# Gated scan and two MLPs on one core: the streamed weights move up by 160 bytes in SBUF

## The chip, the core and the metric

The kernel runs on one core of a Trainium2 chip. The metric is the device time of one execution in microseconds (us), lower is better. PE is the matrix engine (TensorE), PEld its weight loads, DVE the VectorE, ACT the ScalarE, SP the SyncE, whose queue issues the DMAs. SBUF is the on-chip memory of 128 partitions from which the engines read; an address here is a byte offset within each partition. PSUM is the memory of eight banks into which PE sums.

## The reference

```python
# x, f_logit: (2, 6080, 256); lower_bound: (256,); two MLPs with w_in (256, 2048), w_out (2048, 256)
sig = 1.0 / (1.0 + np.exp(-f_logit))
f = lower_bound + (1.0 - lower_bound) * sig
h[t] = f[:, t] * h[t - 1] + (1.0 - f[:, t]) * x[:, t]        # the scan: y[:, t] = h[t]
...
y1 = np.maximum(y @ w_in1, 0.0) ** 2 @ w_out1                # 12160 tokens
h2 = y1 @ w_in2
out = np.where(h2 > 0.0, h2, np.exp(np.minimum(h2, 0.0)) - 1.0) @ w_out2
```

## The kernel before

The 12160 tokens are cut into 12 units: the first of 512 + 384 tokens, the second of 512 + 512, ten more of 512 + 512. A unit is scanned, goes through MLP 1 (m = 0), is written to DRAM (`xd`), read back and goes through MLP 2 (m = 1) two units later. The work of one unit in one MLP is a run; a run has eight slots, one for each group g of 256 of the 2048 inner columns.

All products are of fp32 accuracy from fp32r parts: each operand is split into a high and a low part, and a product is three matmuls, high x high, high x low, low x high (`three`, lines 631 to 636). The first two units of MLP 1 take a slot as plain products, 12 matmuls for each half of the unit (`add_plain`). All later runs save an eighth of the input products with a seven-product scheme for blocks of two by two: `add_first` issues three products (9 matmuls, right operand `xa`), `add_later` four (12 matmuls, right operand `xb`), and ACT and DVE add the results up into `r`. Every matmul of an input product is at line 633, its left operand (the weights) lies in a tile `ws`, which for the seven products holds 2 parts x 7 blocks x 128 columns of fp32 in each partition, 7168 bytes. The pool of `ws` has two buffers; a tile is loaded for each slot by one DMA of 896 KB from the DRAM copy `wd` (`add_stream`, line 472). In the plain slots the weights stand alternately in a `ws` tile (its first four blocks) and in a tile of the pool `s` (`plain_weights`, line 323).

The second product of each MLP, the output sums (line 855), has its weights in SBUF for good: `wo[m]`, 32768 bytes a partition each. Its right operand is `g`, the activated `r`, split by ACT (line 673) and DVE (line 678). A slot of the seven-product runs is therefore four blocks on PE: 9 matmuls of c from xa and ws, 12 of a from g and wo, 12 of c from xb and ws, 12 of a from g and wo, 45 in all; nearly all have 512 columns, the runs of MLP 2's first unit 448.

The order of the work on each engine is fixed when the program is built: the class `Order` plays it through with estimated durations and due times and writes the instructions in that order. Addresses play no part in it. PE's order of blocks comes from `pe_order`. In PSUM each of the four accumulators c0 to c3 has one bank: the next slot's product may begin once ACT or DVE have read the last one (c3 by line 804, `mid_even`).

SBUF is laid out by the order in which the pools are opened, one behind the other, every buffer rounded up to a multiple of 32 bytes. The first 1152 bytes belong to a scratch area and to four constants that every program has. Behind them stood so far the two `ws` buffers, then the pool `const` with five small tiles (lb, ga, gb, carry of 8 bytes, warm of 4) and the two `wo`, then the other pools. lb, ga, gb, carry and warm are the lower bound, the two coefficients of the gate, the state carried between scans and a tile that serves to load a table at the start.

Of the kernel before, what the change touches and what calls it, by code (L numbers as in the profile page):

```python
# [8 lines left out]
F32R = mybir.dt.float32r  # L9
# [6 lines left out]
P = 128  # L16
# [10 lines left out]
BUFS = {  # L27
# [3 lines left out]
}  # L31
# [119 lines left out]
def kernel(  # L151
# [12 lines left out]
    B, S, D = x.shape  # L164
# [3 lines left out]
    KF = DFF // P  # L168
# [6 lines left out]
    PLAIN = len(SIZES)  # L175
    starts = [sum(map(sum, units[:u])) for u in range(NU)]

    pools = {"ws": ctx.enter_context(tc.tile_pool(name="ws_pool", bufs=BUFS["ws"]))}
    const = ctx.enter_context(tc.tile_pool(name="const", bufs=1))
    lb = const.tile([P, KD], F32, name="lb")  # L180
    ga = const.tile([P, KD], F32, name="ga")
    gb = const.tile([P, KD], F32, name="gb")
    carry = const.tile([P, KD], F32, name="carry")
    warm = const.tile([P, 1], F32, name="warm")
    wo = [const.tile([P, KF, 2, D], F32R, name=f"wo{m}") for m in range(2)]
    pools |= {
        tag: ctx.enter_context(tc.tile_pool(name=f"{tag}_pool", bufs=n))
        for tag, n in BUFS.items()
# [67 lines left out]
    for s in slots:  # L256
        m, u, h, g = s
# [702 lines left out]
    for kind, s in pe_order:  # L960
# [3 lines left out]
        m, u, h, g = s  # L964
# [52 lines left out]
```

## Time and profile before

| | |
|---|---|
| median of three runs | 2049.47 us (2049.08 to 2049.62) |
| the profiled execution | 2049.94 us, its span 2048.2 us |
| mean granted PE clock | 0.993 |
| busy share of the span: PE, DVE, ACT | 97%, 82%, 80% |
| DMA | 267.30 MB, 131 GB/s over the span |

The page and the views come from one profiled execution. Times are counted from the start of its span. A row of the timeline merges equal instructions that follow each other: its start, the time from there to the end of the last one, and their number (x12). Matmuls are pipelined, so the end of a block overlaps the start of the next; the time that a block takes on PE is the distance from its start to the next start. Releasers of waits are inferred from semaphore events.

### The profile page before, as it was taken

How to read it: one execution, taken by the hardware profiler on the slowest of the kernel's cores; microseconds unless marked ns; L12 is line 12 of the kernel's file. 1: busy time of each engine (PE TensorE's matmuls, PEld its weight loads, DVE VectorE, ACT ScalarE, POOL GpSimd, SP SyncE). 2: the span in 40 equal slices, each digit the busy share in tenths (PEclk: the TensorE clock that was granted, in tenths of full speed). 3: DMA queues.
4: the chain of work that ended last, by engine and by line, in shares of the span. 5: the costliest groups of instructions: out<-in, count | busy, mean ns of one | idle time of the engine just before them, and what ended most of it. 6: DMA issues, size and time to landing. Idle time of an engine off the chain costs nothing.

```text
span 2048.2 us, 24509 instructions
## 1 busy us (share of the span) xinstructions
PE 1995.6 (97%) x8688; PEld 1633.5 (80%) x8688; DVE 1676.1 (82%) x2285; ACT 1638.2 (80%) x2170; POOL 0.2 (0%) x4
## 2 busy tenths in 40 slices
PE   5999969999999999999999999999999999999998
PEld 4887958888888888888888888888888888888886
DVE  6878997788889779879878888977987987857886
ACT  6988967887888788888788788878888878878885
POOL 0000000000000000000000000000000000000000
PEclk9999989999999999999999999999999999999999
DMA  7877744324324334333432432433433333233231
GB/s 191 240 245 241 230 129 128 131 91 142 125 94 137 99 132 131 111 131 114 128 131 90 143 125 93 137 99 131 132 110 132 114 108 131 91 111 118 94 105 54
DMA packets 235138, 267.30 MB, mean 131 GB/s; under 512 B 160008, under 2 KB 160776, under 8 KB 235016
## 3 DMA queue, kind: packets, MB, share of 16 engines
q1 hardware_dynamic: 234432, 265.21, 41.3%
q8 instruction: 68, 1.11, 0.2%
q10 hardware_dynamic: 584, 0.53, 0.1%
q14 instruction: 54, 0.44, 0.1%
HBM read 221.91 MB, written 43.78 MB: 130 GB/s over the span
## 4 chain that ended last, share of the span: by engine, by line
PE 90%; DVE 4%; ACT 2%; DMA 2%; issue 1%; SPq 1%; DVEq 0%; ACTq 0%
PE a L855 47%; PE c L633 43%; DVE g L678 1%; DMA a<-rd 1%; DMA fs<-in_f_logit_dram 1%; ACT g L673 1%; SPq L566 0%; ACT r L658 0%; ACT a L369 0%; DMA st<-in_moe_w_in_dram 0%; ACT r L725 0%; DVE a L375 0%; DVE a L378 0%; DVE F L602 0%; DVE a L339 0%
## 5 line engine op out<-in xcount | busy, mean ns | idle before, releaser
L855 PE MATMUL a<-g,wo 128*128 128x512 f32 (+1 forms) x4608 | 1107.1, 389 | 0.9 <-DVE g L678 0.9
L855 PEld LDWEIGHTS a<-g,wo 128*128 128x128 f32 x4608 | 865.2, 188 | 184.5 <-DVE g L678 1.3
L678 DVE TENSOR_TENSOR g<-r,g 128x1024 fp32r<-128x1024 f32 (+2 forms) x384 | 463.2, 1206 | 169.4 <-ACT g L673 168.4
L633 PE MATMUL c<-xb,ws 128*128 128x512 f32 (+2 forms) x2208 | 540.4, 393 | 0.0
L673 ACT ACTIVATE g<-r 128x1024 fp32r<-128x1024 f32 (+2 forms) x384 | 403.4, 1050 | 134.7 <-PE a L855 121.8
L633 PEld LDWEIGHTS c<-xb,ws 128*128 128x128 f32 x2208 | 414.7, 188 | 94.2
L633 PE MATMUL c<-xa,ws 128*128 128x512 f32 (+1 forms) x1680 | 427.6, 398 | 44.2 <-ACT xa L482 35.7
L633 PEld LDWEIGHTS c<-xa,ws 128*128 128x128 f32 x1680 | 318.1, 190 | 122.1 <-ACT xa L482 36.1
L756 ACT ACTIVATE s<-c 128x512 f32<-128x512 f32 (+1 forms) x528 | 307.3, 588 | 7.3 <-PE c L633 7.3
L668 DVE SCALAR_TENSOR_TENSOR r<-e,r 128x1024 f32<-128x1024 f32 (+1 forms) x192 | 232.1, 1209 | 34.3 <-ACT e L665 34.3
L662 ACT ACTIVATE e<-r 128x1024 f32<-128x1024 f32 (+1 forms) x192 | 201.5, 1049 | 39.8 <-DVE r L800 37.0
L658 ACT ACTIVATE r<-r 128x1024 f32<-128x1024 f32 x192 | 201.7, 1051 | 2.3
L665 ACT ACTIVATE e<-e 128x1024 f32<-128x1024 f32 (+1 forms) x192 | 201.4, 1049 | 1.5
L796 ACT ACTIVATE r<-c 128x512 f32<-128x512 f32 (+1 forms) x176 | 104.0, 591 | 106.1 <-PE c L633 106.0
L760 DVE TENSOR_TENSOR s<-s 128x512 f32<-128x512 f32 (+1 forms) x176 | 119.9, 681 | 74.2 <-ACT s L756 74.0
L793 DVE TENSOR_TENSOR s<-c,s 128x512 f32<-128x512 f32 (+1 forms) x176 | 120.6, 685 | 39.9 <-PE c L633 38.9
L804 DVE TENSOR_TENSOR r<-c,s 128x512 f32<-128x512 f32 (+1 forms) x176 | 119.5, 679 | 4.4
L800 DVE TENSOR_TENSOR r<-c,s 128x512 f32<-128x512 f32 (+1 forms) x176 | 119.8, 680 | 2.2
L807 DVE TENSOR_TENSOR r<-s 128x512 f32<-128x512 f32 (+1 forms) x176 | 119.1, 677 | 0.0
L652 ACT ACTIVATE r<-r 128x1024 f32<-128x1024 f32 x80 | 84.4, 1055 | 3.5 <-DVE r L807 3.5
L655 ACT ACTIVATE r<-r 128x512 f32<-128x512 f32 x80 | 50.4, 630 | 30.7 <-DVE r L800 30.7
L602 DVE TENSOR_TENSOR_SCAN F<-fT,carry,xT 128x256 f32<-128x256 f32 (+2 forms) x94 | 65.3, 723 | 1.2
(47 smaller groups left out, 759.0 us busy)
## 6 DMA issues: line engine op xcount, KB each, us to landing
ws<-wd SPq DMA_DIRECT2D x176, 896.0 KB, 4.9
fs<-in_f_logit_dram SPq DMA_DIRECT2D x184, 64.0 KB, 2.4
xs<-in_x_dram SPq DMA_DIRECT2D x184, 64.0 KB, 2.5
xd<-o SPq DMA_DIRECT2D x46, 256.0 KB, 4.3
F<-xd SPq DMA_DIRECT2D x22, 512.0 KB, 5.0
out_dram<-o SPq DMA_DIRECT2D x88, 128.0 KB, 2.8
st<-in_moe_w_out_dram SPq DMA_DIRECT2D x16, 512.0 KB, 5.5
wd<-wp SPq DMA_DIRECT2D x24, 256.0 KB, 3.6
```

Source lines behind the costliest of these rows:

```text
L633: nc.tensor.matmul(out, lhsT=ws[:, p, w], rhs=xs[:, r, v], start=start and q == 0, stop=stop and q == 2, skip_group_check=check,)
L658: nc.scalar.activation(r_t[0], r_t[0], AF.Square)
L662: nc.scalar.activation(t["e"], r_t[0], AF.Relu, scale=-1.0)
L665: nc.scalar.activation(t["e"], t["e"], AF.Exp, scale=-1.0)
L668: nc.vector.scalar_tensor_tensor(r_t[0], t["e"], 1.0, r_t[0], op0=ALU.subtract, op1=ALU.max)
L673: nc.scalar.activation(g_t[s, which][:, 0], r_t[0], AF.Copy)
L678: nc.vector.tensor_tensor(g_t[s, which][:, 1], r_t[0], g_t[s, which][:, 0].bitcast(F32), op=ALU.subtract)
L756: nc.scalar.activation(t["s"][:, c - 1], t[c], AF.Copy)
L760: nc.vector.tensor_tensor(t["s"][:, 1], t["s"][:, 1], t["s"][:, 2], op=ALU.add)
L793: nc.vector.tensor_tensor(t["s"][:, 0], t[0], t["s"][:, 0], op=ALU.add)
L800: nc.vector.tensor_tensor(odd[0][:, 1], t[2], t["s"][:, 0], op=ALU.add)
L855: nc.tensor.matmul(a, lhsT=y, rhs=v, start=begin and jj == 0 and p == 0, stop=end and jj == len(mine) - 1 and p == 2, skip_group_check=True,)
```

## The change

The pool of the five small tiles is opened ahead of the pool of `ws`, and the two `wo` get a pool of their own (`outer`) behind it. All pools and tiles keep their sizes and numbers of buffers.

```diff
-    pools = {"ws": ctx.enter_context(tc.tile_pool(name="ws_pool", bufs=BUFS["ws"]))}
     const = ctx.enter_context(tc.tile_pool(name="const", bufs=1))
     lb = const.tile([P, KD], F32, name="lb")
     ga = const.tile([P, KD], F32, name="ga")
     gb = const.tile([P, KD], F32, name="gb")
     carry = const.tile([P, KD], F32, name="carry")
     warm = const.tile([P, 1], F32, name="warm")
-    wo = [const.tile([P, KF, 2, D], F32R, name=f"wo{m}") for m in range(2)]
+    pools = {"ws": ctx.enter_context(tc.tile_pool(name="ws_pool", bufs=BUFS["ws"]))}
+    outer = ctx.enter_context(tc.tile_pool(name="outer", bufs=1))
+    wo = [outer.tile([P, KF, 2, D], F32R, name=f"wo{m}") for m in range(2)]
```

On every engine and queue the instructions and their order stay the same; only the line numbers behind the change are higher by one (L633 becomes L634). The byte addresses of the built programs:

| tile | before | after | rest of division by 64, before | after |
|---|---|---|---|---|
| lb, ga, gb, carry, warm | 15488 to 15647 | 1152 to 1311 | 0 or 32 | the same |
| ws, first buffer | 1152 | 1312 | 0 | 32 |
| ws, second buffer | 8320 | 8480 | 0 | 32 |
| wo, m = 0 and 1 | 15648, 48416 | the same | 32 | 32 |
| xa, xb | 113952, 126240 | the same | 32 | 32 |
| g, two buffers | 167200, 175392 | the same | 32 | 32 |
| s, two buffers | 183584, 189728 | the same | 32 | 32 |

Divided by 512, ws leaves 128 before and 288 after; wo, xa, xb, g and s leave 288.

## Rows read from the trace of the kernel before

**Rows 1.** The page, part 1: busy time, share of the span and instructions of each engine.

```profile
PE 1995.6 (97%) x8688; PEld 1633.5 (80%) x8688; DVE 1676.1 (82%) x2285; ACT 1638.2 (80%) x2170; POOL 0.2 (0%) x4
```

**Rows 2.** Windows: length, busy us (x count) by engine, PEclk, DMA share, GB/s.

```profile
20.00:290.00 270.00, 245.83 (x1113) 210.81 (x1114) 232.58 (x394) 224.62 (x352) 0.00 (x0) 0.96 0.73 221
290.00:2034.00 1744.00, 1744.00 (x7553) 1418.47 (x7552) 1427.79 (x1865) 1406.95 (x1810) 0.00 (x0) 1.00 0.37 117
```

**Rows 3.** Waits of PE: line, releaser, total us, times, longest.

```profile
PE c L633 <- ACT xa L482: 35.7, 2, 20.6
```

**Rows 4.** Timeline of PE, one steady slot: start, us, line, tiles, shapes, count.

```profile
1045.40 2.97 PE L633 MATMUL c<-xb,ws 128*128 128x512 f32 x12
1048.21 2.90 PE L855 MATMUL a<-g,wo 128*128 128x512 f32 x12
1050.94 2.26 PE L633 MATMUL c<-xa,ws 128*128 128x512 f32 x9
1053.04 2.92 PE L855 MATMUL a<-g,wo 128*128 128x512 f32 x12
1055.80 0.86 PE L633 MATMUL c<-xb,ws 128*128 128x512 f32 x3
```

**Rows 5.** Groups by form, PE, 290 to 2034 us: count, busy us, mean ns, idle.

```profile
L855 PE MATMUL a<-g,wo 128*128 128x512 f32 x4009 | 971.1, 391 | 0.0
L633 PE MATMUL c<-xb,ws 128*128 128x512 f32 x2005 | 496.3, 396 | 0.0
L633 PE MATMUL c<-xa,ws 128*128 128x512 f32 x1503 | 377.6, 395 | 0.0
```

**Rows 6.** Timeline of PE in the plain products of the second unit.

```profile
140.42 2.88 PE L633 MATMUL c<-xa,s 128*128 128x512 f32 x12
143.14 2.88 PE L855 MATMUL a<-g,wo 128*128 128x512 f32 x12
145.86 2.88 PE L633 MATMUL c<-xb,s 128*128 128x512 f32 x12
...
151.30 2.97 PE L633 MATMUL c<-xa,ws 128*128 128x512 f32 x12
154.11 2.89 PE L855 MATMUL a<-g,wo 128*128 128x512 f32 x12
156.84 2.97 PE L633 MATMUL c<-xb,ws 128*128 128x512 f32 x12
```

**Rows 7.** Timeline of PE in the run of 448 columns.

```profile
220.76 2.57 PE L633 MATMUL c<-xb,ws 128*128 128x448 f32 x12
223.16 2.60 PE L855 MATMUL a<-g,wo 128*128 128x448 f32 x12
225.60 1.97 PE L633 MATMUL c<-xa,ws 128*128 128x448 f32 x9
```

**Rows 8.** DMA issues: count, KB each, median us from issue to landing.

```profile
ws<-wd SPq DMA_DIRECT2D x176, 896.0 KB, 4.9
...
ws<-wd SPq DMA_DIRECT2D x4, 512.0 KB, 5.1
s<-wd SPq DMA_DIRECT2D x4, 512.0 KB, 4.9
```

**Rows 9.** Timeline of SP: the load of ws in the slot of rows 4.

```profile
1048.40 0.52 SPq L472 DMA_DIRECT2D ws<-wd  x1
```

**Rows 10.** Timeline of DVE and PE at the start of a run.

```profile
438.70 1.23 DVE L678 TENSOR_TENSOR g<-r,g 128x1024 fp32r<-128x1024 f32 x1 [2.17 <-ACT g L673]
...
447.80 2.26 PE L633 MATMUL c<-xa,ws 128*128 128x512 f32 x9
448.32 0.68 DVE L804 TENSOR_TENSOR r<-c,s 128x512 f32<-128x512 f32 x1
```

**Rows 11.** The chain that ended last, 255 to 300 us: start, us, what.

```profile
261.74 4.60 DMA fs<-in_f_logit_dram
...
279.74 1.15 DVE xa L485
```

## The prediction

> **What bounds the kernel now.** I read the busy times first: the matmul engine (PE) is busy 97% of the span, DVE and ACT 82% and 80% [rows 1]. Then the stages: from 290 to 2034 us PE is busy in all of the 1744.00 us, with a granted clock of 1.00, the upper of its two levels (2.4 GHz) [rows 2]. PE waits for nothing in that stretch; its one large wait, 35.7 us in two pieces, is for xa in the first 290 us, as PE pauses nowhere after [rows 2, 3]. So from 290 us on the time is the number of matmuls times the spacing of one, and only that spacing, or a new wait, can change it.
>
> The spacing is read from the starts of neighbouring blocks (the duration shown for a block holds the drain of its last matmul, so the next block's start is what counts). One slot of the steady stage, where the two products with streamed weights (ws) alternate with the output sums (weights wo), reads [rows 4]: 12 matmuls with ws from 1045.40 to 1048.21, 2.81 us, 234.2 ns each; 12 with wo to 1050.94, 2.73 us, 227.5 ns; 9 with ws to 1053.04, 2.10 us, 233.3 ns; 12 with wo to 1055.80, 2.76 us, 230.0 ns. All have 512 columns, the same three-matmul pattern, and none waits. The slot is 10.40 us, and the ws blocks are the slow ones.
>
> Is that the left operand's tile or the work around it? The first units answer it, since there the weights stand alternately in ws and in a buffer of the pool s, while the right operand xa is the same tile [rows 6]: 12 matmuls of xa with s take 2.72 us (140.42 to 143.14), the 12 with wo that follow 2.72 us, 12 of xa with ws 2.81 us (151.30 to 154.11), and the 12 with wo behind those 2.73 us. So 226.7 ns is what this chip does with s and with wo, 234.2 ns with ws, and wo loses a little right behind ws. What sets ws apart from s and wo is its address: every tile named here starts at a multiple of 64 bytes plus 32, save the two ws buffers, which start at a multiple of 64.
>
> **The change part by part.** It moves no instruction and adds none: it moves ws up by 160 bytes, to the same remainder as all others, and the five constants to where ws began. Every block of weights lies at a multiple of 512 bytes from its tile's start, so after the change all the left operands have remainder 32 of 64, and indeed the same remainder of 512 as those of s and wo.
>
> Steady stage. It holds 7553 matmuls [rows 2]: 2005 and 1503 with ws and 4009 with wo of 512 columns [rows 5]; the 36 left over are wo's of 448 columns. If all the 7517 run at the 226.7 ns of s and wo [rows 6], and the 36 at 203.3 ns (2.44 us for 12 [rows 7]), the stage takes 7517 x 0.22667 + 36 x 0.2033 = 1711.2 us in place of 1744.0: a gain of **32.8 us**. About 25 us of it are the ws matmuls themselves (3508 x (233.8 - 226.7) ns), the rest is what wo loses behind ws now (a block of 12 takes 2.73 or 2.76 us, not 2.72 [rows 4]). No row shows ws at the new address, so its price is bounded: 226.7 ns, the nearest row, with the same right operands, is the low end; 234.2 ns plus what the other phase costs at 448 columns is the high end. There ws, at its multiple of 64, takes 2.40 us for 12 (200.0 ns) and wo 2.44 us (203.3 ns) [rows 7], so the phase matters in the other direction at that width: about 3 ns more, +10.5 us over 3508 matmuls. I take the low end, since it has the same width, clock and tiles.
>
> What comes late next. PE will be at each place 0.20 us earlier per slot (10.40 against 45 x 0.22667 = 10.20). The tightest place that I find is where DVE frees the PSUM bank of c3: its L804 starts at 448.32 and ends at 449.00, and the third product of the block that starts at 447.80 needs the bank six matmuls later, at 449.20 [rows 10]. The slack is 0.20 us, and it comes back every second run, 10 times. DVE has worked without a pause since 438.70 there, about one slot [rows 10], so this slack goes to about zero: at worst 0.2 us each, and 0.04 us until the matmuls are back at their spacing (2.76 against 2.72 us). 0 to 2.5 us; I take 1.5 us.
>
> Transfers. The five constants are read a few bytes at a time and cost nothing either way. The ws loads keep their sizes and get a start 32 bytes off a multiple of 64. A load of 512 KB into s, with just that remainder, lands in 4.9 us, one into ws in 5.1 us [rows 8], so none is the price. The cover if that is wrong: a load issued at 1048.40 [rows 9] fills a buffer that is first read two slots after 1050.94 less one, at 1061.34, 12.9 us later, against 4.9 us to landing [rows 8]; it could take twice as long without anyone waiting.
>
> Before 290 us. By the program 144 matmuls with ws of 512 columns gain 7.5 ns each (1.1 us) and 168 of 448 columns lose 3 ns (0.5 us). But the chain that ends this stage runs through a load of f_logit at 261.74 and DVE's xa at 279.74 [rows 11], for which PE stands still in the second of its two waits [rows 3]. I take zero, with 1 us either way.
>
> Sum: the profiled execution took 2049.94 us (span 2048.2). 2049.94 - 32.8 + 1.5 = 2018.6; the median of the runs is 0.47 us lower, so **2018 us**. Own range of this case: 2014 (all of it, no new wait, a start that goes well) to 2023.
>
> **The rivals.** *Partial.* The spacing with ws depends on more than the remainder (the gap of 3584 bytes between the high and the low part, where wo has 1024 and s 2048), and the ws matmuls settle no better than wo does behind ws now, at 230.0 ns [rows 4]. For it: that block shows that a spacing between the two exists. Against it: wo and s have different gaps and the same 226.7 ns. Gain 3508 x 3.8 ns = 13 us with wo unchanged: 2036 us.
>
> *No change.* The place in memory has nothing to do with it, and ws is slow because it is also being refilled, or for a reason in the products. Against it: 12 matmuls with ws and 12 with s, with the same x and the same program lines, differ by 0.09 us in the first units [rows 6], where s is refilled as well. Time: 2049 us. The Trainium skill, SBUF — State Buffer, section "Who interferes with whom", gives PE two independent read ports, one for the moving operand and one for the weights, and says that PE and ACT "never wait on anyone"; by that rule an address costs nothing and this rival holds. The trace doesn't agree: 2.81 against 2.72 us.
>
> *Slower.* The slowness at 512 columns comes from something else about ws, and the only thing that the address does is what 448 columns show, where the multiple of 64 is the better one. Then the place is every ws matmul of the steady stage, the price 3 ns, and 3508 of them give +10.5 us: 2060 us. It decides if the spacing with ws, 234.2 ns now, doesn't fall. Against it: at 512 columns s and wo, with the worse remainder of that reading, are faster than ws.
>
> *A new bound.* DVE (82% busy) or ACT becomes what sets the slot. For it: the 0.20 us of slack [rows 10]. Against it: in the steady stage they are busy 1427.79 and 1406.95 of 1744 us [rows 2], so even in 1711 us they have 16% left. It is in the range of the forecast, as its 0 to 2.5 us, at most 5.
>
> **How the numbers follow.** The forecast has 0.76: the same tiles, width and clock are measured side by side, and only gap and place are not. Partial 0.10, no change 0.09, slower 0.05. A measurement of this kernel can tell about 0.2%, 4 us, from no change. Faster is forecast and partial, 0.86; same 0.09; slower 0.05. The forecast's own range would leave more than 2 in 10 out, so the range takes in the partial case as well: 2014 to 2037 us.
>
> **What would show it.** In the changed profile a block of 12 matmuls with ws should take 2.72 us from its start to that of the next, 9 of them 2.04 us, both wo blocks 2.72, the slot 10.20 us, and PE's unbroken stretch should shorten from 1744 to about 1711 to 1713 us with the same 7553 matmuls. At 448 columns the blocks with ws should go from 2.40 to about 2.44 us: this one step says by itself that the remainder is what counts. A wait of c on DVE L804 (L805 there) may appear, some ten times. If ws blocks still take 2.81 us, the reading of the address is wrong; if they take 2.72 us and the time doesn't fall, look for the wait that ate it.

## The result and the profile after

The changed kernel takes 2018.72 us (median of four runs, 2018.05 to 2019.57) against 2049.55 us before (2049.08 to 2051.31): 30.8 us less, a ratio of 0.9848 with a 95% interval of 0.9831 to 0.9865. The forecast was 2018 us.

The page's first part and the row of the steady stage, from the windows of the changed kernel (columns as in [rows 2]):

```profile
PE 1963.1 (97%) x8688; PEld 1630.1 (81%) x8688; DVE 1674.4 (83%) x2285; ACT 1637.9 (81%) x2170; POOL 0.2 (0%) x4
```

```profile
290.00:2002.00 1712.00, 1712.00 (x7547) 1415.40 (x7545) 1424.68 (x1863) 1405.89 (x1808) 0.00 (x0) 1.00 0.37 119
```

PE's busy time fell from 1995.6 to 1963.1 us; DVE's and ACT's stayed within 2 us of what they were [rows 1]. From 290 us on, 7547 matmuls take 1712.00 us, 226.8 ns each, where 7553 took 1744.00 us, 230.9 ns each [rows 2]. That is the whole gain: 7553 matmuls at that rate are 1713.4 us, 30.6 us less than 1744.0.

One steady slot, in the timeline of PE of the changed kernel, answers to [rows 4]:

```profile
1005.48 2.20 PE L634 MATMUL c<-xa,ws 128*128 128x512 f32 x9
1007.52 2.88 PE L856 MATMUL a<-g,wo 128*128 128x512 f32 x12
1010.24 2.88 PE L634 MATMUL c<-xb,ws 128*128 128x512 f32 x12
1012.96 2.88 PE L856 MATMUL a<-g,wo 128*128 128x512 f32 x12
1015.68 2.20 PE L634 MATMUL c<-xa,ws 128*128 128x512 f32 x9
```

From the start of a block to that of the next: 9 with ws 2.04 us (before 2.10), 12 with wo 2.72 (2.76), 12 with ws 2.72 (2.81), 12 with wo 2.72 (2.73). The slot is 10.20 us, and all blocks have one spacing, 226.7 ns. So the blocks with wo, which no one had moved, gained too. At 448 columns, the same view answers to [rows 7]:

```profile
220.10 2.60 PE L634 MATMUL c<-xb,ws 128*128 128x448 f32 x12
222.54 2.59 PE L856 MATMUL a<-g,wo 128*128 128x448 f32 x12
224.97 1.99 PE L634 MATMUL c<-xa,ws 128*128 128x448 f32 x9
```

Here 12 with ws take 2.44 us, where they took 2.40: the new place is the worse one at this width, as forecast.

The new wait came as well. The place of [rows 10], in the timeline of PE, its weight loads and DVE in the changed kernel:

```profile
443.56 2.42 PE L634 MATMUL c<-xa,ws 128*128 128x512 f32 x9
444.27 0.68 DVE L805 TENSOR_TENSOR r<-c,s 128x512 f32<-128x512 f32 x1
445.01 0.53 PEld L634 LDWEIGHTS c<-xa,ws 128*128 128x128 f32 x3 [0.35 <-DVE r L805]
...
445.81 2.44 PE L856 MATMUL a<-g,wo 128*128 128x512 f32 x10
```

The weight load for the third product now waits for DVE's L805, which ends at 444.95, and the block takes 2.25 us instead of 2.04. It does so at ten places, each 0.21 us longer.

The loads of ws, from the DMA issues of the changed kernel, answer to [rows 8] and land within 0.4 us of what they took:

```profile
ws<-wd SPq DMA_DIRECT2D x176, 896.0 KB, 5.0
...
ws<-wd SPq DMA_DIRECT2D x4, 512.0 KB, 4.7
s<-wd SPq DMA_DIRECT2D x4, 512.0 KB, 4.7
```

### The profile page after: what moved, and what is told of

It reads as the page before. It is cut to its first block, busy times and chain, and to the rows that moved or that the text cites. A ratio compares the mean times of both kernels' runs of the same rounds, so it can differ in the third digit from the quotient of the medians.

```text
span 2016.3 us, 24509 instructions
## 1 busy us (share of the span) xinstructions
PE 1963.1 (97%) x8688; PEld 1630.1 (81%) x8688; DVE 1674.4 (83%) x2285; ACT 1637.9 (81%) x2170; POOL 0.2 (0%) x4
## 4 chain that ended last, share of the span: by engine, by line
PE 88%; DVE 4%; DMA 3%; ACT 3%; issue 1%; SPq 1%; ACTq 0%; DVEq 0%
PE a L856 47%; PE c L634 41%; DVE g L679 1%; DMA fs<-in_f_logit_dram 1%; DMA a<-rd 1%; SPq L567 1%; ACT g L674 1%; ACT r L659 0%; ACT r L726 0%; ACT a L370 0%; DVE a L379 0%; DMA st<-in_moe_w_in_dram 0%; DVE a L376 0%; DMA wd<-ws 0%; DMA xs<-in_x_dram 0%
## 5 line engine op out<-in xcount | busy, mean ns | idle before, releaser
L634 PE MATMUL c<-xb,ws 128*128 128x512 f32 (+2 forms) x2208 | 525.7, 387 | 0.0
L634 PEld LDWEIGHTS c<-xb,ws 128*128 128x128 f32 x2208 | 414.0, 188 | 82.1
L634 PE MATMUL c<-xa,ws 128*128 128x512 f32 (+1 forms) x1680 | 418.3, 392 | 43.8 <-ACT xa L483 35.6
L634 PEld LDWEIGHTS c<-xa,ws 128*128 128x128 f32 x1680 | 315.9, 189 | 115.4 <-ACT xa L483 36.1
L805 DVE TENSOR_TENSOR r<-c,s 128x512 f32<-128x512 f32 (+1 forms) x176 | 119.6, 680 | 4.4
```

The costliest lines, as they stand in the source:

```text
L634: nc.tensor.matmul(out, lhsT=ws[:, p, w], rhs=xs[:, r, v], start=start and q == 0, stop=stop and q == 2, skip_group_check=check,)
```

## The experiments

The number was right, but was it for the remainder of 64? In what follows the *difference* is the start of the left operand's tile less that of the right operand's, and its remainder. In the kernel before it is 1152 - 113952 for ws against xa, which leaves 96 when divided by 256 (32 by 64); in the changed kernel it leaves 0 by 512. None of these kernels leaves out any work; only places in SBUF differ. `gap0` and `gap1` are pools of one unused tile, of so many fp32 numbers in each partition. The diffs are against the changed kernel.

**1. ws alone, up by 32 bytes against the kernel before**, the constants behind it.

```diff
+    gap0 = ctx.enter_context(tc.tile_pool(name="gap0", bufs=1))
+    gap0.tile([P, 8], F32, name="gap0")
+    pools = {"ws": ctx.enter_context(tc.tile_pool(name="ws_pool", bufs=BUFS["ws"]))}
     const = ctx.enter_context(tc.tile_pool(name="const", bufs=1))
...
     warm = const.tile([P, 1], F32, name="warm")
-    pools = {"ws": ctx.enter_context(tc.tile_pool(name="ws_pool", bufs=BUFS["ws"]))}
+    gap1 = ctx.enter_context(tc.tile_pool(name="gap1", bufs=1))
+    gap1.tile([P, 8], F32, name="gap1")
     outer = ctx.enter_context(tc.tile_pool(name="outer", bufs=1))
```

> The two ws buffers move up by 32 bytes alone, to 1184 and 8352; the five constants stay behind them, and all tiles from wo on move up by 64 bytes, so that they keep their remainder of 64. Theory A (the left operand's start and the right operand's start must leave the same remainder of 64): a block of 12 matmuls with ws of 512 columns takes 2.72 us, time 2016 to 2021 us. Theory B (the left operand must start at a multiple of 64 plus 32, wherever the right operand starts): the same. Theory C (what counts is that the constants left the place behind ws): 2.81 us and 2047 to 2052 us, as before. Theory D (the remainder that must agree is that of 128, 256 or 512): ws differs from the others there, so 2.81 us or some value between, 2030 to 2052 us.

Measured: 2045.67 us, ratio to before 0.998 (0.9969 to 0.9991). The timeline of PE, one steady slot:

```profile
1001.81 2.96 PE L638 MATMUL c<-xb,ws 128*128 128x512 f32 x12
1004.61 2.91 PE L860 MATMUL a<-g,wo 128*128 128x512 f32 x12
1007.36 2.26 PE L638 MATMUL c<-xa,ws 128*128 128x512 f32 x9
1009.46 2.89 PE L860 MATMUL a<-g,wo 128*128 128x512 f32 x12
```

12 with ws take 2.80 us although both operands leave 32 by 64. So theories A and B as written, and the prediction's reading of the address, are wrong; D, a modulus (the number that one divides by) larger than 64, stands, and so far C too. The difference here leaves 64 by 128 and by 256, 320 by 512.

**2. The constants alone.**

```diff
     const = ctx.enter_context(tc.tile_pool(name="const", bufs=1))
...
     warm = const.tile([P, 1], F32, name="warm")
+    gap0 = ctx.enter_context(tc.tile_pool(name="gap0", bufs=1))
+    gap0.tile([P, 8], F32, name="gap0")
     pools = {"ws": ctx.enter_context(tc.tile_pool(name="ws_pool", bufs=BUFS["ws"]))}
+    gap1 = ctx.enter_context(tc.tile_pool(name="gap1", bufs=1))
+    gap1.tile([P, 8], F32, name="gap1")
     outer = ctx.enter_context(tc.tile_pool(name="outer", bufs=1))
```

> The five constants stand at the lowest addresses, but ws starts at 1344 and 8512, multiples of 64; all tiles from wo on move up by 64 bytes. Theories A, B and D: a block of 12 with ws takes 2.81 us, one steady slot 10.40 us, time 2047 to 2052 us, as before the change. Theory C (the constants): 2.72 us and 2016 to 2021 us.

Measured: 2041.25 us, ratio 0.996 (0.9941 to 0.998). 12 matmuls with ws take 2.79 us, from the timeline:

```profile
1007.22 2.89 PE L860 MATMUL a<-g,wo 128*128 128x512 f32 x12
1009.95 2.95 PE L638 MATMUL c<-xb,ws 128*128 128x512 f32 x12
1012.74 1.52 PE L860 MATMUL a<-g,wo 128*128 128x512 f32 x6
```

The constants stand where the change puts them, and ws is slow: C falls. The time isn't that of before, 8 us better, which no theory had said: ws has another difference (224 by 256), its blocks take 2.79 and 2.10 us, and both blocks with wo 2.73, where one took 2.76.

**3. Everything up by 32 bytes.**

```diff
+    gap0 = ctx.enter_context(tc.tile_pool(name="gap0", bufs=1))
+    gap0.tile([P, 8], F32, name="gap0")
     const = ctx.enter_context(tc.tile_pool(name="const", bufs=1))
...
     warm = const.tile([P, 1], F32, name="warm")
     pools = {"ws": ctx.enter_context(tc.tile_pool(name="ws_pool", bufs=BUFS["ws"]))}
     outer = ctx.enter_context(tc.tile_pool(name="outer", bufs=1))
```

> The changed kernel with everything moved up by 32 bytes: ws, wo, s, xa, xb and g all start at multiples of 64. Theory A (same remainder for left and right operand): every block of 12 keeps 2.72 us, time 2016 to 2021 us. Theory B (the left operand at a multiple of 64 plus 32): now the blocks with wo are slow as well, 2.81 us all, so 7517 matmuls of the steady stage at 234 in place of 226.7 ns add 54 us: 2065 to 2080 us.

Measured: 2017.29 us, ratio 0.9842 (0.9813 to 0.9871). The timeline of PE has all blocks of 12 at 2.72 us:

```profile
1002.19 2.88 PE L858 MATMUL a<-g,wo 128*128 128x512 f32 x12
1004.91 2.20 PE L636 MATMUL c<-xa,ws 128*128 128x512 f32 x9
1006.95 2.88 PE L858 MATMUL a<-g,wo 128*128 128x512 f32 x12
1009.67 2.88 PE L636 MATMUL c<-xb,ws 128*128 128x512 f32 x12
1012.39 1.98 PE L858 MATMUL a<-g,wo 128*128 128x512 f32 x8
```

ws, wo, s, xa, xb and g all start at multiples of 64 now, and nothing is lost: B falls again. It is not the remainder of 64 of either operand by itself that counts, and the difference of the two is left.

**4. xa and xb up by 32 bytes, ws and wo where they were.**

```diff
-    pools |= {
-        tag: ctx.enter_context(tc.tile_pool(name=f"{tag}_pool", bufs=n))
-        for tag, n in BUFS.items()
-        if tag not in IN_PSUM and tag != "ws"
-    }
+    for tag, n in BUFS.items():
+        if tag not in IN_PSUM and tag != "ws":
+            if tag in ("xa", "wp"):
+                gap = ctx.enter_context(tc.tile_pool(name=f"gap_{tag}", bufs=1))
+                gap.tile([P, 8], F32, name=f"gap_{tag}")
+            pools[tag] = ctx.enter_context(tc.tile_pool(name=f"{tag}_pool", bufs=n))
```

The gap behind xb also moves what lies behind it, g and s among it, by 64 bytes in all.

> The changed kernel with the right operands xa and xb alone moved up by 32 bytes, to multiples of 64; ws, wo, s and g keep a remainder of 32. Theory A (same remainder for both operands): the products from xa and xb are slow again, 2.81 us for 12, and wo loses a little behind them, time 2047 to 2053 us, as before the change, though no weight was moved. Theory B (the left operand alone): 2.72 us, 2016 to 2021 us.

Measured: 2045.93 us, ratio 0.9983 (0.9972 to 0.9994), a little below the 2047 expected. The timeline of PE, a steady slot and two blocks of the first units:

```profile
1002.64 2.96 PE L635 MATMUL c<-xb,ws 128*128 128x512 f32 x12
1005.43 2.91 PE L857 MATMUL a<-g,wo 128*128 128x512 f32 x12
1008.18 2.25 PE L635 MATMUL c<-xa,ws 128*128 128x512 f32 x9
```

```profile
140.73 2.95 PE L635 MATMUL c<-xa,s 128*128 128x512 f32 x12
143.52 2.91 PE L857 MATMUL a<-g,wo 128*128 128x512 f32 x12
```

ws and wo were not moved, yet 12 with ws take 2.79 us, and s, the fast one before, takes 2.79 us as well (140.73 to 143.52), because its difference to xa changed. The matmuls of wo take 2.75 us, because g moved by 64 against wo. B falls a third time; A stays, with a modulus that these four leave open.

**5 to 7. Which modulus: ws up by 64, 128 and 256 bytes against the changed kernel.** All tiles from wo on go up by 512. The diff is that with 64; with 128 and 256 the second gap has 384 and 256 bytes.

```diff
     const = ctx.enter_context(tc.tile_pool(name="const", bufs=1))
...
     warm = const.tile([P, 1], F32, name="warm")
+    gap0 = ctx.enter_context(tc.tile_pool(name="gap0", bufs=1))
+    gap0.tile([P, 16], F32, name="gap0")
     pools = {"ws": ctx.enter_context(tc.tile_pool(name="ws_pool", bufs=BUFS["ws"]))}
+    gap1 = ctx.enter_context(tc.tile_pool(name="gap1", bufs=1))
+    gap1.tile([P, 112], F32, name="gap1")
     outer = ctx.enter_context(tc.tile_pool(name="outer", bufs=1))
```

> The changed kernel with ws 64 bytes higher (1376, 8544) and all tiles from wo on 512 bytes higher, so that these keep their remainder of 512, 288; ws leaves 352, a difference of 64. After the first four experiments theory A stands with another modulus: the weights that are loaded and the columns that are streamed meanwhile must agree in the remainder of 128, 256 or 512. All three moduli: a block of 12 with ws is slow here, 2.74 to 2.81 us (wo against g at a difference of -64 took 2.75 us), time 2025 to 2050 us. If 64 were enough after all: 2.72 us and 2017 to 2020 us.

> As before, with ws 128 bytes higher than in the changed kernel and all other remainders of 512 kept. Modulus 128: 2.72 us for 12 with ws, 2017 to 2020 us. Modulus 256 or 512: slow, 2.74 to 2.81 us, 2025 to 2050 us.

> As before, with ws 256 bytes higher than in the changed kernel and all other remainders of 512 kept. Modulus 128 or 256: 2.72 us for 12 with ws, 2017 to 2020 us. Modulus 512: slow, 2.74 to 2.81 us, 2025 to 2050 us.

Measured: 2046.57 us with 64 (ratio 0.9984, 0.9973 to 0.9995), 2054.61 us with 128 (1.0026, 1.0015 to 1.0037), 2018.68 us with 256 (0.9848, 0.9819 to 0.9877). 256 is as good as 0 and 128 is not: the modulus is 256. The steady slot with 256:

```profile
1000.88 2.88 PE L638 MATMUL c<-xb,ws 128*128 128x512 f32 x12
1003.60 2.88 PE L860 MATMUL a<-g,wo 128*128 128x512 f32 x12
1006.32 2.20 PE L638 MATMUL c<-xa,ws 128*128 128x512 f32 x9
```

With 128 the kernel is slower than before and than the 2050 us at most expected, and the timeline shows where:

```profile
1001.70 2.94 PE L860 MATMUL a<-g,wo 128*128 128x512 f32 x12
1004.47 2.96 PE L638 MATMUL c<-xb,ws 128*128 128x512 f32 x12
1007.26 2.92 PE L860 MATMUL a<-g,wo 128*128 128x512 f32 x12
1010.02 2.27 PE L638 MATMUL c<-xa,ws 128*128 128x512 f32 x9
1012.13 2.25 PE L860 MATMUL a<-g,wo 128*128 128x512 f32 x9
```

The blocks with ws take 2.79 and 2.11 us, about what they took before, but those with wo behind them 2.77 and 2.76 us, more than the 2.76 and 2.73 of [rows 4].

**8. ws up by 16 bytes.** A `ws` buffer of 7680 bytes, of which the tile is the part from byte 16 on.

```diff
+    def new_ws():
+        t = new("ws", [P, 2 * NW * P + P], F32R)[:, 4 : 4 + 2 * NW * P]
+        return t.rearrange("p (x w i) -> p x w i", x=2, w=NW)
...
-            return new("ws", [P, 2, NW, P], F32R)[:, :, :4]
+            return new_ws()[:, :, :4]
...
-                ws_t[wk] = new("ws", [P, 2, NW, P], F32R)
+                ws_t[wk] = new_ws()
```

> The changed kernel with ws 16 bytes higher inside a buffer of 7680 bytes; all tiles from wo on are 1024 bytes higher, so their remainders of 512 stay. Theory A with any modulus and no coarser unit: a difference of 16 is a difference, 2.74 to 2.81 us for 12 with ws and 2025 to 2050 us. If addresses count in units of 32 bytes or more, 16 is none: 2.72 us and 2017 to 2020 us.

Measured: 2019.51 us, ratio 0.9852 (0.9823 to 0.9881); 2.72 us for all blocks of 12 with 512 columns. Theory A without a unit falls: 16 bytes are no difference at this width. (At 448 columns 12 with ws take 2.47 us, not 2.44: 221.72 to 224.19 in its timeline.)

**9 to 11. The other differences: 32, 160 and 192**, by the diff of 5 to 7; one run each.

> As the run with 64, with ws 32 bytes higher than in the changed kernel (difference 32 in the remainder of 256), all other remainders kept. Theory A with modulus 256, any difference of 32 or more costs: a block of 12 with ws takes 2.77 to 2.81 us, time 2035 to 2050 us. If only differences of 64 and more cost: 2.72 us, 2017 to 2020 us.

> Difference 160. Theory A: slow, 2.74 to 2.81 us for 12 with ws, 2030 to 2055 us. If the cost depends only on the distance to the next multiple of 256, it is that of the kernel before (difference 96): 2.81 us and 2045 to 2052 us.

> Difference 192. If the cost depends only on the distance to the next multiple of 256, it is that of the run with 64: 2.80 us for 12 with ws, 2043 to 2049 us. If the sign counts too: about 2.75 us, as wo took against g at -64 in the run with xa and xb moved, and 2025 to 2035 us.

Measured: 2044.02, 2055.98 (1 us above its expectation) and 2025.18 us, beside 2049.29 us for the kernel before, whose runs in experiments 5 to 8 lay within 3.3 us of each other. So 32 costs nearly as much as 64, and the cost doesn't go by the distance to the next multiple of 256: 160 is dearer than 96, and 192 much cheaper than 64. The timeline with 192:

```profile
1002.76 2.91 PE L638 MATMUL c<-xb,ws 128*128 128x512 f32 x12
1005.51 2.88 PE L860 MATMUL a<-g,wo 128*128 128x512 f32 x12
1008.23 2.22 PE L638 MATMUL c<-xa,ws 128*128 128x512 f32 x9
```

2.75 us for 12 with ws, and wo keeps its 2.72. It is the 2.75 us that wo took against g at the same difference in experiment 4; s against xa had 32 there and took 2.79 us, as ws does here with 32, and ws had 224 there and took 2.79 us, as in experiment 2. Three pairs of other tiles, three times the same numbers: with 512 columns the difference by 256 tells the spacing of a block, up to what its neighbour adds (a wo block at difference 0 takes 2.72 to 2.77 us).

**12. ws up by 160 bytes against the kernel before, the constants behind it.**

```diff
+    gap0 = ctx.enter_context(tc.tile_pool(name="gap0", bufs=1))
+    gap0.tile([P, 40], F32, name="gap0")
+    pools = {"ws": ctx.enter_context(tc.tile_pool(name="ws_pool", bufs=BUFS["ws"]))}
     const = ctx.enter_context(tc.tile_pool(name="const", bufs=1))
...
     warm = const.tile([P, 1], F32, name="warm")
-    pools = {"ws": ctx.enter_context(tc.tile_pool(name="ws_pool", bufs=BUFS["ws"]))}
+    gap1 = ctx.enter_context(tc.tile_pool(name="gap1", bufs=1))
+    gap1.tile([P, 24], F32, name="gap1")
     outer = ctx.enter_context(tc.tile_pool(name="outer", bufs=1))
```

> ws moves up by 160 bytes as in the change, but the five constants stay behind it; all tiles from wo on move up by 256 bytes, so that their remainder of 256 stays. Theory A with modulus 256: the whole gain, 2.72 us for 12 with ws and 2016 to 2021 us. If the place of the constants has a share in it: between that and 2049 us.

Measured: 2018.11 us, ratio 0.9848 (0.9806 to 0.989). The whole gain comes with ws alone; the constants only served as 160 bytes of filling.

All steady blocks with 512 columns, from start to start in the timelines, by the difference of ws against xa and xb; wo against g leaves 0 in all these rows:

| difference by 256 | run | 12 with ws, us | 12 with wo behind them, us | time, us |
|---|---|---|---|---|
| 0 | the change; 7; 12; 3 | 2.72 | 2.72 | 2018.72; 2018.68; 2018.11; 2017.29 |
| 16 | 8 | 2.72 | 2.72 | 2019.51 |
| 32 | 9 | 2.79 | 2.74 | 2044.02 |
| 64 | 5; 1 | 2.80 | 2.75 | 2046.57; 2045.67 |
| 96 | before | 2.81 | 2.73 | 2049.55 |
| 128 | 6 | 2.79 | 2.76 | 2054.61 |
| 160 | 10 | 2.80 | 2.77 | 2055.98 |
| 192 | 11 | 2.75 | 2.72 | 2025.18 |
| 224 | 2 | 2.79 | 2.73 | 2041.25 |

## Why the prediction was right, and where not

*The bound and the price.* Right: the steady stage was matmuls times spacing, and the spacing with ws became that of s and wo, 226.7 ns. For the 7553 matmuls the forecast had 1711.2 us and 1.5 us of waits, and 1713.4 us is what they take now. Of the two ends of the bound the low one came; that a place can be dearer than the old one is true of others (experiments 6 and 10), but there the blocks with ws take no longer than before, 2.79 and 2.80 us for 12, and those with wo do.

*The wait on DVE.* Right in place, number and kind: L805, ten times. Mis-sized by 0.6 us: 0.21 us each, 2.1 us and not 1.5, near the upper end of 0 to 2.5.

*Transfers and the start.* Right: the loads land within 0.4 us of before, and DVE's xa, which ends the first stage, starts at 279.21 instead of 279.74, inside the 1 us allowed. *448 columns*: 2.44 us, as forecast, but the step does not say "by itself that the remainder is what counts". Experiments 1 and 2 in their timelines:

```profile
220.02 2.59 PE L638 MATMUL c<-xb,ws 128*128 128x448 f32 x12
222.45 2.60 PE L860 MATMUL a<-g,wo 128*128 128x448 f32 x12
...
220.21 2.64 PE L638 MATMUL c<-xb,ws 128*128 128x448 f32 x12
222.69 2.64 PE L860 MATMUL a<-g,wo 128*128 128x448 f32 x12
225.16 2.02 PE L638 MATMUL c<-xa,ws 128*128 128x448 f32 x9
```

In experiment 1 the 12 with ws take 2.43 us, though at 512 columns they are still slow. In experiment 2 ws starts at a multiple of 64, as it did before, and they take 2.48 us, not 2.40.

*What sets ws apart.* The time came, but this step failed: "What sets ws apart from s and wo is its address: every tile named here starts at a multiple of 64 bytes plus 32, save the two ws buffers, which start at a multiple of 64." The address it is, but not that of the left operand alone: it is the difference from the right operand's (experiments 3 and 4). And the remainder of 64 was only the first property in which the tiles differed. Experiment 1 makes this remainder equal and gains 3 us; experiments 5 to 7 show that the two must agree by 256. The number was safe from this error because the change makes the operands agree by 512, which the next paragraph of the prediction had noted. That was luck: moving ws up by 32 bytes, which the same reading would have recommended as well, is experiment 1. The trace of before could not tell the moduli apart: it held one slow difference, 96, and one fast, 0.

*The rivals.* Partial falls: the gap between high and low part is the same 3584 bytes, and the spacing is 226.7 ns. No change falls: experiment 4 slows the matmuls with ws by moving xa and xb, and experiment 12 gives the whole gain by moving ws, so an address does cost on PE. With it falls for this case what the prediction drew from the Trainium skill, SBUF — State Buffer, section "Who interferes with whom": that with two independent read ports an address costs nothing. Slower did not come. Places that are worse than the old one exist, at 128 and 160, but not by its mechanism: it is the blocks with wo that take longer there. A new bound did not come beyond the 2 us on DVE.

*What stays open.* The runs show which differences cost, not why. That it is the weights being loaded for the next matmul against the columns streamed by the current one fits a detail of experiment 2, whose timeline has the last matmul of a wo block at 1009.71 and the next, the first with ws, at 1009.95: 0.24 us for a matmul of wo itself, where the eleven ahead of it took 2.49 us, 0.226 each. But that reading asks for a slow last matmul of the wo block wherever ws is slow, and the traces have it only in part: read over all steady wo blocks, the last matmul has a median of 235, 232, 237 and 235 ns at the differences 32, 128, 160 and 224, but of 226, 228 and 226 ns at 64, 96 and 192, and 227 at 0. No run tested it by itself. Why the first matmuls of a wo block lose time behind ws at most differences, but not at 192 and 224, is open too.

## What to carry to other kernels

When PE is busy without a break, compare the start-to-start time of blocks with the same shape and different tiles; a difference of 3% that follows a tile and not the work can be its place, as here. Then write down the starts of PE's two operands and their difference by 256, not only by the first power of two that separates them, and fill with a few bytes until the width that dominates is fastest; with 512 columns this was at 0 (and 16) of the nine differences measured here. Any change to a pool ahead of them can undo it, and a faster PE can run into the next engine's smallest slack, as it did at ten places here.

## What the runs showed that was not expected

Places that no instruction order shows are worth up to 1.9% here: 2017.29 to 2055.98 us for the same instructions. A difference of 16 bytes costs nothing with 512 columns, one of 32 costs 0.07 us in 12 matmuls. The best difference depends on the width: at 448 columns 96 gives 2.40 us for 12 [rows 7] and 0 gives 2.44. There the difference of a block's own operands is not enough to tell its spacing: a block with wo against g at 0 takes 2.43 us in the changed kernel (222.54 to 224.97) and 2.47 in experiment 2 (222.69 to 225.16). And a bad place also slows the well placed block beside it, by up to 0.05 us in 12 matmuls (2.77 against 2.72 us).
